# An attention-and-MLP kernel on one core: attention output computed token-major, 48 columns a head, and transposed afterwards

## The chip, the cores and the metric

The kernel runs on one core of a Trainium2 chip. Every time is in microseconds (us) on the device. The median of seven runs of the kernel before is 222.66 us (220.71 to 225.13). "PE" is the matrix engine (TensorE) and "PEld" its weight loads, "DVE" the vector engine, "ACT" the scalar engine, "POOL" GpSimd, and "SP" the sync engine, which here only issues DMAs. In a matmul one operand is loaded as weights and the other moves through the array; the number of moving columns is called its width.

## What is computed

There are two parts. The first is a gated linear attention over 4 sequences of 768 tokens, with 8 heads of 48 values; the second is a two-layer MLP with a sine-square activation on the result (d_model 384, d_ff 2048, 3072 tokens).

```python
f = 1.0 / (1.0 + np.exp(-f_logit))
for t in range(S):
    state = f[:, :, t, :, None] * state + np.einsum('bhd,bhe->bhde', k[:, :, t], v[:, :, t])
    y[:, :, t] = np.einsum('bhd,bhde->bhe', q[:, :, t], state)
x = y.transpose(0, 2, 1, 3).reshape(B * S, H * D)
h = x @ w_in
s = np.sin(alpha * h)
g = h + s * s / (alpha + 1e-09)
out = g @ w_out
```

Inputs and outputs are float32; the matmuls take bfloat16.

## The kernel before, in words

**Tiling.** The 768 tokens are cut into 6 chunks `c` of 128. A "unit" `u` is one chunk of two sequences, 12 in all; `m` counts the 24 pairs of chunk and sequence `b`. For each chunk all 4 sequences give one token block of 512 columns for the MLP; in chunk 0 alone the MLP works on two halves of 256.

**The gate phase, `pre` (from L326).** For a unit ACT takes exp and ln of the gate logits (L333, L336). For each `m`, PE sums the logs over tokens with a triangular mask (`cs`, L363 and, for the decay of the whole chunk, L366); ACT takes two exponentials of it (`Gi` L376, `G` L372); POOL or DVE multiplies k and DVE multiplies q (L385) into `qk`. DVE makes `v` bfloat16 (`values`, L342 to L347). exp and ln live in another activation table than the sine, so ACT switches tables (L628) between gate phases and sines; the list `PHASES` says when.

**The attention of a chunk, `attend`.** `tp` (L420) transposes k and q on PE and `tr` (L428) evicts them, in chunks 0 to 3; in chunks 4 and 5 a DMA transpose issued by SP does this (L426). `aps` (L437) is k against q, DVE masks it into `at` (L440). The output y is made of `inter` (L445, the carried state against q) and `intra` (L458, v against `at`); both leave it with **features on partitions**: the weights are the state or v, and the moving operand is 128 tokens wide. Two heads share a matmul and a head is padded from 48 to 64 rows, so the output comes in 4 blocks of 128 rows, and its rows don't lie as the MLP wants them. Hence `v_b` is stored padded, with zeros; `y_` (L465) evicts all 4 blocks into `xT`; and `spread` (L508) moves the fourth block's rows, in pieces of 16 partitions, into gaps of the other three, by 6 small DMAs a chunk from SP or POOL. For chunk 0 a second copy of v (`v1_b`) lets PE do this itself, with 12 matmuls instead of 8. The rows of `w_in` are loaded in the same order, in 16 DMAs (L295). `kv_` (L471, L473) adds the chunk's k times v to the state (the old state is added by an identity matmul, L471), and DVE scales it by the decay into `st` (L479).

**The MLP.** `first` makes h (PE, three matmuls of 512 columns, L529), the sine (ACT, L534), its square (POOL, ACT or DVE, L540 and L542) and g (DVE, L547). `second` sums 16 matmuls of 384 columns into o (L566), evicts it (L574) and stores it (L577).

**Order.** Nothing is left to a scheduler on the chip: `in_order` plans it while the program is built, from each operation's written durations, ranks (`RANK`, `ATT`, `LAG`, `KIND`), engine biases (`BIAS`) and rings of buffers (`R`), and then each engine runs its instructions in exactly that order. The loads follow the list `LOADS`; `W_GATE` names the loads after which POOL issues the weights. PSUM has three rings: 3 buffers for attention (`a`, shared by cs, tp, aps, y and kv), 3 for h, 2 for o. `NG` is the number of g tiles that may wait for o.

Of the kernel before, what the change touches and what calls it, by code (L numbers as in the profile page):

```python
# [17 lines left out]
NG = 36  # L18
PE_TR = 4
SPARE = 15  # L20
LOADS = [("k", 0), ("f", 0), ("q", 0), ("v", 0), ("f", 1), ("v", 1), ("q", 1), ("k", 1), ("f", 3),
    ("k", 3), ("f", 2), ("q", 3), ("q", 2), ("f", 5), ("v", 3), ("v", 2), ("k", 2), ("k", 4),
    ("f", 4), ("v", 4), ("q", 4), ("k", 5), ("v", 6), ("q", 5), ("k", 7), ("v", 7), ("f", 6),
    ("v", 5), ("k", 6), ("f", 7), ("q", 6), ("v", 10), ("f", 8), ("q", 7), ("q", 8), ("k", 8),
    ("v", 8), ("k", 11), ("v", 9), ("v", 11), ("f", 11), ("f", 9), ("k", 9), ("q", 10), ("k",
    10), ("q", 9), ("q", 11), ("f", 10)]
W_GATE = [1, 6, 15]
LAG = [389, 183, 51, 210, 208, 289]
ATT = [150, -130, -181, 58, -47, 55]
PHASES = [("pre", [0]), ("pre", [1]), ("sin", 16), ("pre", [2, 3]), ("sin", 15), ("pre", [4, 5]),  # L30
    ("sin", 17), ("pre", [6, 7, 8]), ("sin", 18), ("pre", [9, 10, 11]), ("sin", 46)]
RANK = [-6, 628, -691, -10, 175, 71, 8, 20, -437, -18, -103, -123]
MULS = {"POOL": 1020, "DVE": 750}
KIND = {"v": [147, 9, 46, 75, 127, -2],
        "cs": [-145, -32, -204, -182, -55, -258],
        "kh": [-179, -112, -104, -31, -147, -299],
        "qh": [-145, -50, -132, -383, -199, -136],
        "tp": [-133, -167, -186, -203, -128, -244],
        "tr": [116, 196, 76, 293, 139, 285],
        "a": [-282, -297, -247, -321, -246, -206],  # L40
        "m": [83, 264, 119, 421, 58, 182],
        "y": [-85, 152, 24, 75, 105, 196],
        "i": [81, 10, -86, -217, 109, 54],
        "kv": [148, 97, 59, 86, 61, 178],
        "st": [129, 130, -157, 126, 215, -54],
        "h": [5, -27, 43, 31, -36, -92],
        "sq": [114, 125, 112, 12, 253, 139],
        "g": [-119, 51, -134, 78, 119, -14],
        "ev": [-69, -174, -183, -117, -240, -203]}
SPREAD = {"SP": 1800, "POOL": 1600}  # L50
BIAS = {"ACT": 400, "DVE": 500, "POOL": 500, "SP": -1800}
# [12 lines left out]
class Op:  # L64
    after, line = 0, None
# [11 lines left out]
def in_order(ops, lines):  # L77
# [28 lines left out]
    while left:  # L106
        best = None
        for o in pending:
            if o.line and turn[o] != nth[o.line]:
                continue  # L110
            t = when(o)
            if t is None:
                continue
            for e, dur in o.engs.items():
                s = max(t, free[e])
                if o.dma:
                    s = max(s, dma_free[e] - DMA_AHEAD)
                d = dur + (TABLE_LOAD if o.table and o.table != table and table else 0)
                key = (s + (BIAS[e] if len(o.engs) > 1 else 0), o.rank, s + d)
                if best is None or key < best[0]:  # L120
                    best = (key, o, e, s, d)
# [28 lines left out]
def kernel(  # L150
# [18 lines left out]


# [3 lines left out]
    E = 64  # L174
# [7 lines left out]
    POS = (0, 3, 1, 2)  # L182
# [28 lines left out]
    def op(rank, engs, emit, deps=(), takes=(), holds=(), table=None, dma=None):  # L211
# [8 lines left out]
        h=N_H, s=3, s2=3, g=NG, o=2, osb=3).items()}  # L220
# [6 lines left out]
    v1_b = [consts.tile([C, 2, 2, 7, E], BF16, name=f"v1{i}") for i in range(2)]  # L227
    v_b = [consts.tile([C, HP, 2, 2, 2, E], BF16, name=f"vb{i}") for i in range(NV)]
# [21 lines left out]
    for i in range(max(NQ, NV)):  # L250
        for ts in (lf_b, v_b, v1_b, qk_b):
            if i >= len(ts):
                continue
            if ts is v_b:
                nc.vector.memset(ts[i], 0.0)
            elif ts is v1_b:
                nc.vector.memset(ts[i], 0.0)
            else:
                nc.vector.memset(ts[i].rearrange("c x y r e -> c (x y r) e")[:, :, D:], 0.0)
# [30 lines left out]
    def w_in_load(hf, rank):  # L290
        gate = weights_after(hf, rank)
        for j, p0, r0, n in ((0, 0, 0, E), (1, 0, 80, E), (2, 16, 3 * D, D), (2, 0, D + 16, 16)):
            for r in range(2):
                def emit(e, j=j, p0=p0, r0=r0, n=n, r=r):
                    nc.gpsimd.dma_start(out=w_in_bf[r * E + p0:r * E + p0 + n, j, HF[hf]],  # L295
                                        in_=moe_w_in[4 * D * r + r0:4 * D * r + r0 + n, HF[hf]])
                w_in_dma[hf].append(op(rank, {POOL: 550}, emit, deps=[gate],
                                       dma=830 if n == E else 620 if n == D else 210))
# [27 lines left out]
    def pre(u, rank):  # L326
        c = u // NU
# [11 lines left out]
        def values(e):  # L339
            vi = tl["v", u].rearrange("c (br p) d -> c p br d", p=HP)  # L340
            vo = v_b[bufs["vb", u].place % NV].rearrange("c p b r x e -> c p (b r) x e")
            nc.vector.tensor_copy(vo[:, 0:2, :, 0, :D], vi[:, 0:2])  # L342
            nc.vector.tensor_copy(vo[:, 2:4, :, 0, 16:], vi[:, 2:4])
            if u < NU:
                v1 = v1_b[u].rearrange("c b r x e -> c (b r) x e")
                nc.vector.tensor_copy(v1[:, :, 1, D:], vi[:, 1, :, :16])
                nc.vector.tensor_copy(v1[:, :, 3:6:2, :16], vi[:, 1, :, 16:].rearrange("c n (x d) -> c n x d", x=2))  # L347
# [4 lines left out]
        made["v", u] = op(rank + KIND["v"][c] + 2, {DVE: 1300 if u < NU else 1050}, values, deps=[vb_.ready], takes=[vv], holds=[vb_])  # L352
        late = []
        for i in range(2):
# [34 lines left out]
            c_ = op(rank + KIND["cs"][c] + i, {PE: 170 if last else 370}, cs_, deps=[l], takes=[cb], holds=[lf])  # L389
# [7 lines left out]
            made["kh", m] = op(rank + KIND["kh"][c] + i, MULS, km, deps=[gi, kb_.ready], takes=[qkb], holds=[kb_, Gib])  # L397
            made["qh", m] = op(rank + KIND["qh"][c] + i, {DVE: 490}, qm, deps=[g, qb_.ready], takes=[qkb], holds=[qb_, cb])
# [5 lines left out]
    def attend(c, b, rank):  # L404
        u, i = c * NU + b // 2, b % 2
        m = 2 * u + i
        first, last = c == 0, c == NCH - 1
        tpb, trb, ab, atb = c < PE_TR and buf("a"), buf("tr"), [buf("a"), buf("a")], [buf("at0"), buf("at1")]
        yb, kvb, sb = buf("a"), buf("a"), buf(f"st{b}")
# [31 lines left out]

        def inter_(e):
            y = tl[x, "y"] = ps_a.tile([P, HP, C], F32, tag="a", name=f"y_{c}_{b}")
            for p in range(HP):
                nc.tensor.matmul(y[:, POS[p], :], tl["st", c - 1, b][:, p, :, :].rearrange("d r e -> d (r e)"),  # L445
                                 tl[x, "tr"][:, HP + p, :], start=(p == 0), stop=False, skip_group_check=True)

        def intra_(e, r):
            if first and r == 0:
                tl[x, "y"] = ps_a.tile([P, HP, C], F32, tag="a", name=f"y_{c}_{b}")  # L450
            for p in range(HP):
                if first and p == 1:
                    v1 = v1_b[u][:, i, r].rearrange("c x e -> c (x e)")
                    vs = [(blk, v1[:, (2 * n + 1 - r) * E:(2 * n + 3 - r) * E]) for n, blk in enumerate((0, 2, 1))]
                else:
                    vs = [(POS[p], v_b[vb.place % NV][:, p, i].rearrange("c r x e -> c (r x e)")[:, r * E:(r + 2) * E])]
                for blk, v_ in vs:
                    nc.tensor.matmul(tl[x, "y"][:, blk, :], v_, tl[x, "at", r][:, p, :],  # L458
                                     start=(first and p == r == 0), stop=(r == 1), skip_group_check=True)

        def y_(e):
            if ("xT", c) not in tl:
                tl["xT", c] = xp.tile([P, HP, TOK], BF16, tag="xT", name=f"xT_{c}")
            n = KB if first else HP
            (nc.scalar.copy if e == ACT else nc.vector.tensor_copy)(  # L465
                tl["xT", c][:, :n, b * C:(b + 1) * C], tl[x, "y"][:, :n, :])

        def kv_(e):
            kv = tl[x, "kv"] = ps_a.tile([P, HP, 2, E], F32, tag="a", name=f"kv_{c}_{b}")
            if not first:  # L470
                nc.tensor.matmul(kv, ident, tl["st", c - 1, b], start=True, stop=False, skip_group_check=True)  # L471
            for p in range(HP):
                nc.tensor.matmul(kv[:, p, :, :], qk_b[qkb.place % NQ][:, 0, p, :, :].rearrange("c r e -> c (r e)"),  # L473
                                 v_b[vb.place % NV][:, p, i, :, 0, :],
                                 start=(first and p == 0), stop=True, skip_group_check=True)

        def st_(e):
            t = tl["st", c, b] = st_pool.tile([P, HP, 2, E], BF16, tag=f"s{b}", name=f"st_{c}_{b}")
            nc.vector.tensor_tensor(t, tl[x, "kv"], tl["gl", m].unsqueeze(3).to_broadcast([P, HP, 2, E]),  # L479
                                    Alu.mult)  # L480

        if c < PE_TR:
            kt = op(rank + KIND["tp"][c], {PE: 250}, lambda e: tp_(e, 0), deps=[made["kh", m]], takes=[tpb], holds=[qkb])
# [176 lines left out]
```

## Time and profile before

| | us |
|---|---|
| Median of seven runs | 222.66 |
| The profiled execution, its own time | 220.65 |
| Its span, first to last instruction | 218.9 |
| PE busy (85%), as the profile models ends | 187.1 |
| ACT busy (75%) | 165.1 |
| DVE busy (75%) | 164.5 |
| POOL busy (45%) | 99.6 |

The granted PE clock was 0.967 of full speed on average. The inputs are read in 48 loads of 384 KB by SP; they take most of the first 130 us. A busy share of PE counts the latency of each matmul, and so overstates how full PE is: the pitch, from one matmul's start to the next, is used below instead. The lines of the profile stand in the prediction.

### The profile page before, as it was taken

Reading aid. Unit: us, or ns where it says so; the run is one execution under the profiler, and the core shown is the slowest. Engines: PE = TensorE matmul, PEld = TensorE weight load, DVE = VectorE, ACT = ScalarE, POOL = GpSimd, SP = SyncE. Lnnn points to the kernel's source line nnn. Section 1 sums busy time; section 2 is a strip of 40 time slices with the busy share of each in tenths; the row PEclk is TensorE's granted clock in tenths of the full one; section 3 lists DMA queues with packets and bytes.
Section 4 is the critical chain, followed back from the end, with each engine's and each line's share of the span. In section 5 each row is a group of like instructions: output and inputs, shape, how many; then the busy total and the mean of one; then the engine's idle time right before and its main releaser. Section 6 shows DMA issues by size and latency. Waiting matters only on the chain.

```text
span 218.9 us, 4306 instructions
## 1 busy us (share of the span) xinstructions
PE 187.1 (85%) x1513; PEld 115.3 (53%) x1529; DVE 164.5 (75%) x301; ACT 165.1 (75%) x275; POOL 99.6 (45%) x134
## 2 busy tenths in 40 slices
PE   0259774888999898986899999999999999999993
PEld 0157552566675455643565654655665555555551
DVE  7677778568987999894589898669878858778700
ACT  2545949987689787899968889988877787777511
POOL 5721776176427454854633355465454642132300
PEclk9999999569999999999699999999999999999999
DMA  8999999999993999969699996555410101101111
GB/s 132 191 211 188 189 209 185 192 180 201 190 174 77 179 190 187 182 131 214 146 198 189 180 157 116 167 144 99 96 55 7 72 18 39 55 17 43 68 72 72
DMA packets 115125, 29.61 MB, mean 135 GB/s; under 512 B 108720, under 2 KB 114336, under 8 KB 115104
## 3 DMA queue, kind: packets, MB, share of 16 engines
q1 hardware_dynamic: 111648, 26.04, 67.0%
q0 software_dynamic: 3456, 3.30, 9.1%
q8 instruction: 12, 0.20, 0.4%
q14 instruction: 9, 0.07, 0.1%
HBM read 25.17 MB, written 4.72 MB: 137 GB/s over the span
## 4 chain that ended last, share of the span: by engine, by line
PE 57%; ACT 11%; DMA 10%; DVE 7%; SPq 5%; issue 5%; POOL 2%; ACTq 0%; POOLq 0%
PE o L566 24%; PE h L529 21%; SPq L271 5%; DMA q<-in_q_dram 4%; DMA w_out_bf<-in_moe_w_out_dram 3%; PE y L458 3%; DVE g L547 3%; DMA w_in_bf<-in_moe_w_in_dram 3%; ACT f L333 3%; PE aps L437 2%; ACT Gi L376 2%; PE y L445 2%; ACT L628 2%; POOL w_in_bf L295 2%; PE tp L420 2%
## 5 line engine op out<-in xcount | busy, mean ns | idle before, releaser
L542 POOL TENSOR_TENSOR s<-s 128x512 f32<-128x512 f32 (+1 forms) x65 | 58.5, 911 | 69.7 <-ACT s L534 57.9
L534 ACT ACTIVATE s<-h,al_p 128x512 f32<-128x512 f32 (+1 forms) x112 | 67.6, 628 | 25.3 <-PE h L529 22.8
L529 PE MATMUL h<-xT,w_in_bf 128*128 128x512 bf16 (+1 forms) x320 | 77.1, 355 | 6.7 <-DVE g L547 3.1
L547 DVE SCALAR_TENSOR_TENSOR g<-s,al_r,h 128x512 bf16<-128x512 f32 (+1 forms) x112 | 71.9, 665 | 12.4 <-POOL s L542 9.3
L566 PE MATMUL o<-w_out_bf,g 128*128 128x384 bf16 x384 | 78.1, 329 | 1.1 <-DMA w_out_bf<-in_moe_w_out_dram 1.1
L566 PEld LDWEIGHTS <-g 128*128 128x128 bf16 x384 | 36.5, 98 | 25.3 <-issue 1.6
L529 PEld LDWEIGHTS <-w_in_bf 128*128 128x128 bf16 x336 | 32.2, 100 | 29.7 <-issue 5.0
L440 DVE TENSOR_TENSOR at<-aps,mask 128x512 bf16<-128x512 f32 x48 | 31.4, 683 | 3.5 <-PE aps L437 3.2
L385 POOL TENSOR_TENSOR qk<-k,Gi 128x384 bf16<-128x384 f32 x22 | 21.6, 1002 | 17.7 <-ACT Gi L376 17.7
L540 ACT ACTIVATE s<-s 128x512 f32<-128x512 f32 (+1 forms) x36 | 20.8, 584 | 0.9
L385 DVE TENSOR_TENSOR qk<-q,cs 128x384 bf16<-128x384 f32 x24 | 13.2, 552 | 10.1 <-ACT cs L372 10.0
L363 PE MATMUL cs<-lf,mask 128*128 128x384 bf16 x24 | 9.0, 381 | 12.3 <-ACT lf L336 10.1
L458 PE MATMUL y<-at,vb 128*128 128x128 bf16 x184 | 18.5, 228 | 0.3 <-DVE at L440 0.3
L479 DVE TENSOR_TENSOR st<-kv,gl 128x512 bf16<-128x512 f32 x20 | 13.3, 683 | 5.4 <-PE kv L473 5.4
L420 PE MATMUL tp<-ident,qk 128*128 128x128 bf16 x128 | 12.1, 250 | 3.7 <-POOL qk L385 2.0
L574 ACT COPY osb<-o 128x384 f32<-128x384 f32 x16 | 7.7, 479 | 9.4 <-PE o L566 9.2
L333 ACT ACTIVATE f<-f 128x768 f32<-128x768 f32 x12 | 10.0, 836 | 5.9 <-POOL seen L287 5.1
L458 PEld LDWEIGHTS <-vb 128*128 128x128 bf16 x184 | 13.1, 103 | 2.4 <-issue 0.2
L376 ACT ACTIVATE Gi<-cs 128x384 f32<-128x384 f32 x24 | 11.6, 484 | 3.4 <-PE cs L366 2.7
L437 PE MATMUL aps<-tr 64*128 64x128 bf16 x192 | 10.5, 229 | 4.2 <-DVE tr L428 3.0
L420 PEld LDWEIGHTS <-qk 128*128 128x128 bf16 x128 | 9.9, 113 | 6.9 <-POOL qk L385 3.8
L465 ACT CAST xT<-y 128x512 bf16<-128x512 f32 (+1 forms) x20 | 11.2, 566 | 1.5 <-PE y L458 1.2
(56 smaller groups left out, 171.1 us busy)
## 6 DMA issues: line engine op xcount, KB each, us to landing
k<-in_k_dram SPq DMA_DIRECT2D x12, 384.0 KB, 6.6
f<-in_f_logit_dram SPq DMA_DIRECT2D x12, 384.0 KB, 6.7
q<-in_q_dram SPq DMA_DIRECT2D x12, 384.0 KB, 6.7
v<-in_v_dram SPq DMA_DIRECT2D x12, 384.0 KB, 6.8
out_dram<-osb SPq DMA_DIRECT2D x24, 192.0 KB, 1.9
w_out_bf<-in_moe_w_out_dram POOLq DMA_DIRECT2D x4, 384.0 KB, 7.6
w_in_bf<-in_moe_w_in_dram POOLq DMA_DIRECT2D x8, 128.0 KB, 5.5
w_in_bf<-in_moe_w_in_dram POOLq DMA_DIRECT2D x4, 96.0 KB, 6.2
```

The source lines that it names most:

```text
L333: nc.scalar.activation(out=tl["f", u], in_=tl["f", u], func=Act.Exp, scale=-1.0)
L376: nc.scalar.activation(out=tl["Gi", m], in_=tl["cs", m][:, :H * D], func=Act.Exp)
L385: engine[e].tensor_mul(qk_b[bufs["qk", m].place % NQ][:, "kq".index(n), :, :, :D], tl[n, u][:, i * H:(i + 1) * H, :].rearrange("c (r p) d ...
L420: nc.tensor.transpose(tl[x, "tp"][:, j * HP + p, :], qk_b[qkb.place % NQ][:, j, p, :, :].rearrange("c r e -> c (r e)"), ident)
L440: nc.vector.tensor_mul(tl[x, "at", r], tl[x, "a"][r], mask4)
L458: nc.tensor.matmul(tl[x, "y"][:, blk, :], v_, tl[x, "at", r][:, p, :], start=(first and p == r == 0), stop=(r == 1), skip_group_check=True)
L529: nc.tensor.matmul(h[:, :n], w_in_bf[:, kb, fs], xT[:, kb, ts], start=(kb == 0), stop=(kb == KB - 1))
L534: nc.scalar.activation(out=s[:, :n], in_=tl[x, "h"][:, :n], func=Act.Sin, scale=al_p[:, fb:fb + 1])
L540: nc.scalar.activation(out=s2[:, :n], in_=s[:, :n], func=Act.Square)
L542: engine[e].tensor_mul(s2[:, :n], s[:, :n], s[:, :n])
L547: nc.vector.scalar_tensor_tensor(tl["g", c, fb][:, ts], tl[x, "s2"][:, :n], al_r[:, fb:fb + 1], tl[x, "h"][:, :n], Alu.mult, Alu.add)
L566: nc.tensor.matmul(tl["o", c, t], tl["g", c, fb][:, t * P:(t + 1) * P], w_out_bf[:, fb, :], start=(fb == 0), stop=(fb == FB - 1))
```

## The change

The output of attention is now computed with **tokens on partitions**: `at` and the transposed q (`tr`) are the weights, and v (48 columns) or the state (96 columns, two heads) moves. A head needs no padding: v is one contiguous copy (`v_b` with H x 48 columns), the zeroing of `v_b` and `v1_b` at the start is gone, and so is `v1_b`. y is one tile of 128 x 384, evicted to `yn`. It must then be transposed for the MLP: in chunks 0 to 2 (`Y_TR = 3`) by three PE transposes into a PSUM buffer of ring `a` and an eviction `x_` by DVE or ACT, in chunks 3 to 5 by a DMA transpose from SP. x is in natural order, so `spread` is gone and `w_in` comes in 6 plain DMAs.

The state has 48 columns a head too. From chunk 2 on (`SUM = 2`) the identity matmul is gone: DVE adds the old state (`sum_`), and the scaling goes to POOL or DVE.

The numbers for the planner are all new, with values for each unit where there was one for each chunk, a bias for ACT (`ON_ACT`), another order of loads, another gate for weights, 44 g tiles in place of 36, and one gate phase more (that of units 6 to 8 is cut in two). In the instruction order of the built program POOL does all 12 scalings of the state that it may do, and ACT has 12 table loads where there were 10.

```diff
-NG = 36
+NG = 44
 PE_TR = 4
+Y_TR = 3
+SUM = 2
...
-W_GATE = [1, 6, 15]
+W_GATE = [4, 7, 14]
...
-PHASES = [("pre", [0]), ("pre", [1]), ("sin", 16), ("pre", [2, 3]), ("sin", 15), ("pre", [4, 5]),
-    ("sin", 17), ("pre", [6, 7, 8]), ("sin", 18), ("pre", [9, 10, 11]), ("sin", 46)]
+PHASES = [("pre", [0]), ("pre", [1]), ("sin", 18), ("pre", [2, 3]), ("sin", 14), ("pre", [4, 5]),
+    ("sin", 10), ("pre", [6]), ("sin", 6), ("pre", [7, 8]), ("sin", 16), ("pre", [9, 10, 11]),
+    ("sin", 48)]
...
-    v1_b = [consts.tile([C, 2, 2, 7, E], BF16, name=f"v1{i}") for i in range(2)]
-    v_b = [consts.tile([C, HP, 2, 2, 2, E], BF16, name=f"vb{i}") for i in range(NV)]
+    v_b = [consts.tile([C, 2, H, D], BF16, name=f"vb{i}") for i in range(NV)]
...
-            if ts is v_b:
-                nc.vector.memset(ts[i], 0.0)
-            elif ts is v1_b:
-                nc.vector.memset(ts[i], 0.0)
...
+        for kb in range(KB):
+            def emit(e, kb=kb):
+                nc.gpsimd.dma_start(out=w_in_bf[:, kb, HF[hf]], in_=moe_w_in[kb * P:(kb + 1) * P, HF[hf]])
...
+            nc.vector.tensor_copy(v_b[vv.place % NV].rearrange("c b h d -> c (b h) d"), tl["v", u])
...
         def inter_(e):
-            y = tl[x, "y"] = ps_a.tile([P, HP, C], F32, tag="a", name=f"y_{c}_{b}")
+            y_tile()
+            y = tl[x, "y"].rearrange("c (r p d) -> c p r d", r=2, p=HP)
             for p in range(HP):
-                nc.tensor.matmul(y[:, POS[p], :], tl["st", c - 1, b][:, p, :, :].rearrange("d r e -> d (r e)"),
-                                 tl[x, "tr"][:, HP + p, :], start=(p == 0), stop=False, skip_group_check=True)
+                nc.tensor.matmul(y[:, p], tl[x, "tr"][:, HP + p, :], tl["st", c - 1, b][:, p, :, :],
+                                 start=(p == 0), stop=False, skip_group_check=True)
         def intra_(e, r):
...
+                h = HP * r + p
+                nc.tensor.matmul(tl[x, "y"][:, h * D:(h + 1) * D], tl[x, "at", r][:, p, :],
+                                 v_b[vb.place % NV][:, i, h, :],
+                                 start=(first and p == r == 0), stop=(r == 1), skip_group_check=True)
...
+        def yt_(e):
+            if e == SP:
+                nc.sync.dma_start_transpose(xT(e), tl[x, "yn"].rearrange("c k d -> c (k d)"))
+                return
+            tl[x, "yt"] = ps_a.tile([P, KB, C], BF16, tag="a", name=f"yt_{c}_{b}")
+            for kb in range(KB):
+                nc.tensor.transpose(tl[x, "yt"][:, kb, :], tl[x, "yn"][:, kb, :], ident)
+        def x_(e):
+            (nc.scalar.copy if e == ACT else nc.vector.tensor_copy)(xT(e), tl[x, "yt"])
...
-            if not first:
+            if not first and c < SUM:
                 nc.tensor.matmul(kv, ident, tl["st", c - 1, b], start=True, stop=False, skip_group_check=True)
...
+        def sum_(e):
+            t = tl[x, "sum"] = at_pool.tile([P, HP, 2, D], F32, tag="sum", bufs=2, name=f"sum_{c}_{b}")
+            nc.vector.tensor_tensor(t, tl[x, "kv"], tl["st", c - 1, b], Alu.add)
+        def st_(e):
+            t = tl["st", c, b] = st_pool.tile([P, HP, 2, D], BF16, tag=f"s{b}", name=f"st_{c}_{b}")
+            engine[e].tensor_tensor(t, tl[x, "kv"] if c < SUM else tl[x, "sum"],
+                                    tl["gl", m].unsqueeze(3).to_broadcast([P, HP, 2, D]), Alu.mult)
...
-    def spread(c, rank):
-        def emit(e, r):
-            xT = tl["xT", c]
-            for blk, dst, src in ((0, D, 0), (2, 0, 16), (1, 0, 32)):
-                engine[e].dma_start(out=xT[r * E + dst:r * E + dst + 16, blk, :],
-                                    in_=xT[r * E + src:r * E + src + 16, 3, :])
...
+                nc.tensor.matmul(h[:, :n], w_in_bf[:, kb, fs], xT[:, ts.start // C:ts.stop // C, kb, :],
                                  start=(kb == 0), stop=(kb == KB - 1))
```

## The prediction

> **What bounds the kernel now.** I read the page's busy shares first, then the three rows of engines over 40 slices, then stretches cut at ACT's table switches, and last PE's order of time in the late part.
>
> ```profile
> PE   0259774888999898986899999999999999999993
> DVE  7677778568987999894589898669878858778700
> ACT  2545949987689787899968889988877787777511
> PE 57%; ACT 11%; DMA 10%; DVE 7%; SPq 5%; issue 5%; POOL 2%; ACTq 0%; POOLq 0%
> ```
>
> No engine is full for the whole span. From slice 21 (115 us) on PE is; before it ACT and DVE take turns. The chain that ended last says the same: 57% PE, most of it late. The stretches (length, then busy us of PE, PEld, DVE, ACT, POOL, granted clock, DMA, GB/s):
>
> ```profile
> 0.00:35.65 35.65, 19.46 (x177) 14.63 (x177) 26.09 (x61) 20.54 (x38) 19.41 (x46) 1.00 1.22 187
> 35.65:62.55 26.90, 21.70 (x209) 15.79 (x210) 20.27 (x45) 21.18 (x40) 12.70 (x20) 0.81 1.27 193
> 62.55:95.08 32.53, 30.25 (x278) 18.51 (x280) 30.10 (x51) 27.84 (x43) 17.75 (x20) 1.00 0.98 162
> 95.08:133.50 38.42, 34.26 (x286) 20.35 (x289) 30.78 (x59) 33.93 (x55) 18.76 (x22) 0.96 0.99 177
> 133.50:145.80 12.30, 12.25 (x91) 7.20 (x90) 8.20 (x17) 11.51 (x21) 6.34 (x8) 1.00 0.50 132
> 145.80:218.90 73.10, 69.14 (x479) 38.87 (x484) 49.09 (x72) 50.10 (x81) 24.59 (x24) 0.99 0.19 56
> ```
>
> PE's busy time includes latency, so I take pitches from its order of time (start, length, count):
>
> ```profile
> 159.01 0.40 PE L437 MATMUL aps<-tr 64*128 64x128 bf16 x8
> 159.34 0.40 PE L445 MATMUL y<-tr,st 128*128 128x128 bf16 x4
> 159.58 0.61 PE L458 MATMUL y<-at,vb 128*128 128x128 bf16 x8
> 160.03 0.81 PE L529 MATMUL h<-xT,w_in_bf 128*128 128x512 bf16 x3
> 160.67 0.39 PE L445 MATMUL y<-tr,st 128*128 128x128 bf16 x4
> 162.64 1.30 PE L566 MATMUL o<-w_out_bf,g 128*128 128x384 bf16 x7
> 163.78 0.81 PE L529 MATMUL h<-xT,w_in_bf 128*128 128x512 bf16 x3
> ```
>
> From one start to the next: h 0.64/3 = 0.214 us (other places 0.216, which I use), o 1.14/7 = 0.1625, y of L458 0.45/8 = 0.056, aps 0.33/8 = 0.041. With these, all PE work is 170 us. The last mask matmul `cs` starts at 144.49; what PE has after it is 129 h x 0.216, 208 o x 0.1625, 56 aps x 0.041, 101 narrow ones x 0.056 and a few wide: 69.9 us. PE's last matmul ends at 215.3, so 70.8 us passed. PE is the bound there, within 1 us.
>
> Before that it isn't: PE has 99.9 us of work in 144.5. ACT's instructions, counted in order with their mean durations, make 123.2 us to the end of its last gate phase at 145.8: 22.6 us of idle, of which 13.3 lie before the first switch back at 35.65. After it ACT idles 9.3 us in 110. So stage 1 (to 144.5) is ACT's, with the start; stage 2 (70.8) PE's; then an eviction and a store (3.6), and 1.75 outside the span.
>
> **The change, stage 1.** *ACT* in the new order, to the same point: 2 table loads more (+2.6), 1 `tr` more (+1.0), evictions of y 15 x 0.484 in place of 3 x 0.484 and 10 x 0.581 (0), 4 evictions of transposes (rows: 0.484 for 384 f32 columns, 1.011 for 1024 bf16; I take 0.48: +1.9), 2 sines fewer (-1.4), 9 squares fewer (-4.6: they go to POOL or past this point), 5 evictions of o fewer (-2.4, to DVE). Sum -2.9: 120.3.
>
> *The start.* exp of the gates began when the second load had landed:
>
> ```profile
> 7.18 0.84 ACT L333 ACTIVATE f<-f 128x768 f32<-128x768 f32 x1 [5.08 <-POOL seen L287]
> ```
>
> Now f is the first load. 384 KB at 190 GB/s are 2.0 us: -2.0. The zeroing of v (4 x 0.912 + 2 x 0.805 = 5.2 us of DVE) ran to 7.8, beside the wait for the load; gone, it leaves DVE free when an earlier load needs it, so it is no second gain. The first half of `w_in` now waits for the 5th load in place of the 2nd, but by issues of 3 x 0.6 us in place of 8 x 0.5; I expect it near 21 us, as the first h needs it now (21.46), and the second half near 29 (30.77). Cost 0, up to +2 if late.
>
> *The new step* from y to x in chunk 0: 3 transposes at 0.056 with a latency near 0.25, then an eviction (DVE: between 0.26, in proportion to 0.682 for 1024 bf16, and 0.557 for 384 f32; I take 0.35) with a wait at each end: about +1.0 once before the first sines. In chunks 1 and 2 the sines of the chunk before cover it.
>
> *Idle after the start.* DVE's work to the same point falls from 128.4 to about 117: zeroing -5.2; v copies 24 in two kinds (0.58 on average, and the `v1_b` copies) to 12 of about 0.75, -5.7; state steps 20 x 0.683 to 18 x 0.55 so far, -3.8 (12 scalings go to POOL at 1.0, the row of its 384-column multiply; the state is needed a chunk later, so that is covered); x +2.1; o evictions +2.2; others -1. PE's work falls from 99.9 to 95.3. ACT waits for PE's h, which waits for buffers that DVE frees (ACT waited for h 19 times in 36 to 146 us, 9.8 us in all). Bounds: 0 to -5 of the 9.3; I take a quarter, -2.2.
>
> One v copy rests on a rule. The Trainium skill ("SBUF — State Buffer", section on the two sides) says that DVE in a two-port mode and GpSimd hold a shared port for a whole instruction, and the other blocks. The trace agrees, and prices it:
>
> ```profile
> 11.13 1.02 POOL L385 TENSOR_TENSOR qk<-k,Gi 128x384 bf16<-128x384 f32 x1
> 11.25 1.14 DVE L342 CAST vb<-v 128x384 bf16<-128x384 f32 x1
> 12.31 0.35 DVE L343 CAST vb<-v 128x384 bf16<-128x384 f32 x1
> ```
>
> Two equal copies, 1.14 beside POOL's multiply and 0.35 after it. Twice the columns[...] add 0.2: 0.55 alone, and 1.3 if each meets a POOL instruction. POOL gets 12 state scalings more. At the bad end the copies give back 12 x 0.55 = 6.6 us of DVE, and my -2.2 with it.
>
> Stage 1: -2.9 - 2.0 + 1.0 - 2.2 = -6.1, so 138.4. Could the loads forbid it? SP's last load left at 128.7; to 130 us the core moved 23.1 MB, at 195 GB/s 118 us of it. Twelve us of slack.
>
> **Stage 2.** After its last `cs` the new PE order has 135 h, 204 o, 48 aps, 48 of `intra`, 24 of `inter`, 8 of kv; two chunks of y, the last `kv` included. Widths are 48 and 96. For 96 columns I scale to 0.0425. For 48 the ends are: 0.056 (no gain), and 0.025, the pitch of the one-column matmuls:
>
> ```profile
> 99.91 0.24 PE L366 MATMUL cs<-ones_c,lf 128*128 128x1 bf16 x4
> ```
>
> (one lasts 0.164, so 0.076 for three steps). I take 0.041, as aps has a weight load for each matmul at that pitch. Sum: 29.2 + 33.2 + 2.0 + 2.0 + 1.0 + 0.5 = 67.8 us, -2.1; over the whole kernel 163.1 for 169.8, of which the 12 identity matmuls fewer give 2.8 and the 36 transposes take 2.0. A rule speaks against this: the Trainium skill ("TensorE: Matmul & The Clock Gate", section on LDWEIGHTS) prices a load at its columns over 1.2 GHz, 107 ns for 128, whatever the width that follows. Then 192 `intra` matmuls would take 20.5 us and not 7.9: +12.6, of which 48 x 0.066 = 3.2 in stage 2. But the rows above show 128-column loads every 0.041 and 0.056 us, so I hold to the row.
>
> DVE has more in stage 2: 57.2 us for 51.5 (4 o evictions, 3 y, 2 g, 2 sums more). Before, the 51.5 took 61.6 us to its last g, 10 idle, and PE ran on for 7 us behind it. With 1.1 after the last g, 56 in about 61 leave 5 idle: +0.7. The DMA transposes of chunks 3 to 5 (issue 1.26, landing 3.2 for 1024 columns, 384 here) stand in place of `spread`'s six issues (3.7 for six, landing 1.8); SP has little else to do then, and h of the chunk before covers them: 0. Stage 2: -1.4, so 69.4.
>
> **Sum.** 138.4 + 69.4 + 3.6 + 1.75 = 213.2 against the profiled 220.65. The median stands 2.0 above that: **215.2**.
>
> **Rivals.**
> *The idle goes away* (0.18). ACT's 9.3 us fall to about 2, with -5 more than I take, since both engines that it waits for are relieved. Then 210. For: DVE at 30.1 of 32.5 in 62 to 95 us. Against: gate phases have idle of their own ("issue", 0.4 us at a time).
> *Nothing gained before stage 2* (0.13). ACT's order hardly changes its work, and if v copies and the later weights eat the start, only -1.4 stays: 221, or 223 with one late weight.
> *PSUM's ring becomes the bound: slower* (0.17). Ring `a` still has 3 buffers, now with a 7th user per chunk and sequence in chunks 0 to 2. A transposed y holds one until DVE or ACT, both in fixed order, evict it; `cs`, `tp` and `aps` queue on PE behind that, and ACT's gate phase behind `cs`. At 1 us for each of 12 that is +12: 227. It decides from 7.4/12 = 0.6 us each. For: DVE's queue is near full just there. Against: the v and state steps leave it.
>
> **How the numbers follow.** Main case 0.52, 212 to 219. A difference below 0.5% (1.1 us) is about what this kernel's times can't tell from none. Faster: main, the first rival and half of the second, 0.76; within 0.5%: 0.07; slower 0.17. Range: 209 leaves under a tenth below; 225 takes in the lesser stalls of the ring.
>
> **What would show it.** exp starting near 5.2; the last `cs` at 138 to 139 and PE's end 69 us later; `intra` of eight matmuls in 0.33 us (0.45 or 0.85 would be the other two prices); evictions of `yt` below 0.5 us on DVE; v copies of 0.55 at their least. Wrong if the last `cs` comes after 144, or if PE shows idle time on `yt`'s eviction.

## The result, and the profile after

The changed kernel takes 218.94 us (median of 12 runs, 217.36 to 221.07); the kernel before, beside it, 222.51. The ratio is 0.986 (95% interval 0.9825 to 0.9895): 1.4% faster, where 3.3% was forecast. 218.9 lies in the range, but 3.7 us above the 215.2. Medians take in every execution; ratios, here and below, leave out the slow ones (one of the 12 here, three of six in `w_dve`), so the two can differ.

The two traces differ by less than the medians: the profiled execution of after took 220.5 us (span 218.8), near the slow end of its runs, and that of before 220.65, at the fast end of its runs. So stretches are compared one by one below, and whole kernels by their medians and ratios.

The rows of engines over 40 slices and the chain that ended last, of after:

```profile
PE   0468646736999988896999989997999999999993
DVE  2387862737689579988969998749899968787820
ACT  3565443897479997698998898998898888687601
PEclk9999975885799999999999999999999999999999
PE 52%; ACT 13%; DVE 9%; DMA 9%; POOL 6%; SPq 5%; issue 5%; ACTq 0%; POOLq 0%
```

and the row of the granted PE clock of before:

```profile
PEclk9999999569999999999699999999999999999999
```

Late in the span little has changed. What is new stands in the 5th to 7th digit (22 to 38 us): ACT at 4, 4 and 3 where it was at 9, 4 and 9, PE at 6, 4 and 6 where it was at 7, 7 and 4, and a clock of 7 and 5 from the 6th digit on. The dip at 5 and 7 further on (49 to 60 us) is not new: before has one at 5 and 6, two slices earlier. In the chain PE has lost 5 points, POOL has gained 4, ACT and DVE 2 each. The stretches, cut at ACT's table switches as before (start:end, length, then busy us of PE, PEld, DVE, ACT, POOL, granted clock, DMA share, GB/s):

```profile
0.00:41.65 41.65, 22.49 (x199) 15.97 (x200) 23.96 (x59) 21.38 (x40) 17.79 (x39) 0.88 1.17 179
41.65:146.28 104.63, 92.04 (x879) 55.64 (x879) 83.33 (x158) 90.67 (x147) 62.20 (x71) 0.95 1.06 176
144.97:215.25 70.28, 68.97 (x470) 36.90 (x467) 53.90 (x83) 52.27 (x85) 21.52 (x22) 1.00 0.22 60
```

and the last two of them for the kernel before, whose first stretch (0 to 35.65) the prediction shows:

```profile
35.65:145.80 110.15, 98.46 (x859) 61.85 (x869) 89.34 (x169) 94.45 (x158) 55.55 (x67) 0.94 1.00 171
144.49:215.30 70.81, 70.44 (x489) 39.74 (x494) 50.21 (x74) 50.92 (x84) 25.72 (x25) 1.00 0.19 55
```

That is the result in five rows. The gate phases (second stretch) became 5.5 us shorter, as forecast. Stage 2 became 0.5 shorter. And the first stretch, forecast at 34.7, became 41.65: ACT has only 0.8 us more work in it and 5.2 us more idle time than before. Where that idle time ends is in the order of time of POOL, PE and ACT, of after:

```profile
24.66 0.17 POOL L286 COPY seen<-v 1x1 f32<-1x1 f32 x1 [5.83 <-DMA v<-in_v_dram]
24.78 0.60 POOL L293 DMA_DIRECT2D w_in_bf<-in_moe_w_in_dram  x1
25.39 0.89 POOL L556 TENSOR_TENSOR s<-s 128x256 f32<-128x256 f32 x1
26.24 0.59 POOL L293 DMA_DIRECT2D w_in_bf<-in_moe_w_in_dram  x1
26.85 0.62 POOL L556 TENSOR_TENSOR s<-s 128x256 f32<-128x256 f32 x1
27.41 0.59 POOL L293 DMA_DIRECT2D w_in_bf<-in_moe_w_in_dram  x1
...
33.99 0.40 PE L543 MATMUL h<-xT,w_in_bf 128*128 128x256 bf16 x1 [3.70 <-DMA w_in_bf<-in_moe_w_in_dram]
35.33 5.70 PE L543 MATMUL h<-xT,w_in_bf 128*128 128x256 bf16 x28 [0.94 <-DMA w_in_bf<-in_moe_w_in_dram]
...
26.32 0.47 ACT L548 ACTIVATE s<-h,al_p 128x256 f32<-128x256 f32 x1 [2.50 <-POOL s L556]
...
35.82 0.47 ACT L548 ACTIVATE s<-h,al_p 128x256 f32<-128x256 f32 x1 [5.19 <-PE h L543]
```

and of before:

```profile
21.01 0.17 POOL L287 COPY seen<-q 1x1 f32<-1x1 f32 x1 [8.86 <-DMA q<-in_q_dram]
21.25 4.10 POOL L295 DMA_DIRECT2D w_in_bf<-in_moe_w_in_dram  x8
...
30.77 0.61 PE L529 MATMUL h<-xT,w_in_bf 128*128 128x256 bf16 x4 [1.28 <-DMA w_in_bf<-in_moe_w_in_dram]
```

The second half of `w_in` waits, on POOL, for a load that marks when it may go. That was q1, the 7th load, seen at 21.01. Now it is v1, the 8th, seen at 24.66. The squares of the sines stand in POOL's order behind that copy and between the three issues. The gate opens 3.65 us later. The three issues, with the squares between them, take 3.2 us where the eight took 4.1, so the last one leaves 2.65 us later (28.0 in place of 25.35). And from there to PE's last wait for `w_in` it is 7.3 us in place of 5.4: the rows of `w_in` needed by block 8 arrive at 33.99 to 35.33 in place of 30.77. PE stands still for 3.70 us. ACT stands still twice: 2.50 us for a square that had to wait behind the copy on POOL, and 5.19 us for h.

The delay then grows, by PE's clock. Windows of after and, last, of the run `a_quarters` below (columns as above):

```profile
30.00:34.00 4.00, 0.30 (x2) 0.01 (x1) 1.38 (x4) 0.60 (x2) 0.00 (x0) 0.93 1.02 169
35.33:41.03 5.70, 5.70 (x28) 4.02 (x29) 3.75 (x9) 4.03 (x9) 3.88 (x7) 0.55 1.29 195
```

```profile
32.57:34.20 1.63, 1.59 (x13) 1.28 (x14) 0.31 (x1) 1.31 (x4) 0.76 (x2) 1.00 0.85 174
```

The 28 matmuls that had been held up ran at 0.204 us each, with a granted clock of 0.55; the same shape took 0.122 (13 in 1.59) at a clock of 1.00 in `a_quarters`, where PE's wait just before them was 1.37 us. 28 x 0.08 = 2.3 us is my estimate of what the clock cost, as ACT's last ten sines of the chunk went at PE's pace; no run takes the clock alone. The Trainium skill ("TensorE: Matmul & The Clock Gate", Part 1 on the clock gate) says the clock is halved after an idle window of about 3.4 us; the 3.70 us here fit it. But these traces show no such threshold: in after the clock was at 0.50 from 27 to 30 us too, behind a wait of 1.86 us.

### The profile page after: what moved, and what is told of

The parts are those of the page before. It is cut to its first block, busy times and chain, and to the rows that moved or that the text cites. A ratio compares the mean times of both kernels' runs of the same rounds, so it can differ in the third digit from the quotient of the medians.

```text
span 218.8 us, 4284 instructions
## 1 busy us (share of the span) xinstructions
PE 182.2 (83%) x1537; PEld 107.7 (49%) x1537; DVE 160.4 (73%) x297; ACT 163.5 (75%) x269; POOL 100.2 (46%) x129
## 4 chain that ended last, share of the span: by engine, by line
PE 52%; ACT 13%; DVE 9%; DMA 9%; POOL 6%; SPq 5%; issue 5%; ACTq 0%; POOLq 0%
PE o L581 23%; PE h L543 21%; DMA v<-in_v_dram 5%; SPq L270 5%; DVE g L561 4%; POOL s L556 4%; DMA w_in_bf<-in_moe_w_in_dram 4%; ACT L643 3%; ACT s L548 3%; ACT Gi L364 2%; DVE at L429 2%; PE aps L426 2%; ACT lf L331 1%; ACT f L328 1%; PE tp L409 1%
## 5 line engine op out<-in xcount | busy, mean ns | idle before, releaser
L543 PE MATMUL h<-xT,w_in_bf 128*128 128x512 bf16 (+1 forms) x336 | 79.5, 362 | 9.8 <-DMA w_in_bf<-in_moe_w_in_dram 4.8
L543 PEld LDWEIGHTS <-w_in_bf 128*128 128x128 bf16 x336 | 33.1, 102 | 36.7 <-issue 7.1
L581 PEld LDWEIGHTS <-g 128*128 128x128 bf16 x384 | 35.8, 98 | 23.5 <-issue 0.7
L351 PE MATMUL cs<-lf,mask 128*128 128x384 bf16 x24 | 8.1, 357 | 10.0 <-ACT lf L331 8.6
L446 PE MATMUL y<-vb,at 128*128 128x48 bf16 x192 | 11.5, 187 | 5.0 <-DVE vb L335 3.1
L446 PEld LDWEIGHTS <-at 128*128 128x128 bf16 x192 | 8.9, 98 | 11.2 <-DVE at L429 5.2
L426 PE MATMUL aps<-tr 64*128 64x128 bf16 x192 | 11.0, 228 | 2.6 <-ACT tr L417 1.5
L556 DVE TENSOR_TENSOR s<-s 128x512 f32<-128x512 f32 (+1 forms) x11 | 7.8, 708 | 7.2 <-ACT s L548 7.1
L417 ACT COPY tr<-tp 128x1024 bf16<-128x1024 bf16 x10 | 9.9, 1019 | 3.9 <-PE tp L409 3.9
L409 PEld LDWEIGHTS <-qk 128*128 128x128 bf16 x128 | 10.4, 118 | 4.9 <-POOL qk L373 2.6
```

The costliest lines, as they stand in the source:

```text
L409: nc.tensor.transpose(tl[x, "tp"][:, j * HP + p, :], qk_b[qkb.place % NQ][:, j, p, :, :].rearrange("c r e -> c (r e)"), ident)
L446: nc.tensor.matmul(tl[x, "y"][:, h * D:(h + 1) * D], tl[x, "at", r][:, p, :], v_b[vb.place % NV][:, i, h, :], start=(first and p == r == 0 ...
L543: nc.tensor.matmul(h[:, :n], w_in_bf[:, kb, fs], xT[:, ts.start // C:ts.stop // C, kb, :], start=(kb == 0), stop=(kb == KB - 1))
L556: engine[e].tensor_mul(s2[:, :n], s[:, :n], s[:, :n])
L581: nc.tensor.matmul(tl["o", c, t], tl["g", c, fb][:, t * P:(t + 1) * P], w_out_bf[:, fb, :], start=(fb == 0), stop=(fb == FB - 1))
```

## The experiments

| run | what it is | us | ratio to before (95%) | second switch | last `cs` |
|---|---|---|---|---|---|
| before | | 222.5 to 223.1 | 1 | 35.65 | 144.49 |
| after | | 218.94 | 0.986 (0.9825 to 0.9895) | 41.65 | 144.97 |
| `a_unsplit` | after, three issues together | 218.31 | 0.9805 (0.9753 to 0.9857) | 39.94 | 142.34 |
| `a_gate` | after, gate q1, issues together | 216.27 | 0.9731 (0.9681 to 0.9781) | 38.46 | 140.86 |
| `a_quarters` | after, gate q1, in two parts | 215.32 | 0.9661 (0.9628 to 0.9693) | 36.56 | 140.08 |
| `b_late` | before, second half of `w_in` late | 227.09 | 1.0203 (1.0151 to 1.0255) | 41.34 | 149.71 |
| `layout_old_numbers` | new layout, planner's numbers of before | 244.65 | 1.0983 (1.0926 to 1.104) | | |
| `w_wide` | after, narrow matmuls twice | 221.94 | 0.9965 (0.9937 to 0.9993) | 41.54 | 146.31 |
| `w_memset` | after, zeroing put back | 220.89 | 0.9915 (0.9886 to 0.9943) | 42.41 | 145.73 |
| `w_dve` | after, zeroing and more v copies | 222.75 (218.93 to 225.99) | 0.9898 (0.984 to 0.9957) | 39.95 | 144.91 |
| `q_memset` | `a_quarters`, zeroing put back | 215.62 | 0.9719 (0.9661 to 0.9777) | 34.87 | 138.32 |
| `q_copy` | `a_quarters`, more v copies | 218.82 | 0.9851 (0.9787 to 0.9915) | 37.42 | 142.22 |

The last two columns are of each run's profiled execution.

My theory: the new layout gives what was forecast, and the late second half of `w_in` takes half of it away. The rivals: the start is late for another reason (DVE, or loads), or the layout's gain is small.

**The gate alone.** `a_unsplit` keeps the gate v1 and only takes the squares from between the issues:

```diff
-                nc.gpsimd.dma_start(out=w_in_bf[:, kb, HF[hf]], in_=moe_w_in[kb * P:(kb + 1) * P, HF[hf]])
+                for j in [kb] if hf == 0 else range(KB) if kb == 0 else []:
+                    nc.gpsimd.dma_start(out=w_in_bf[:, j, HF[hf]], in_=moe_w_in[j * P:(j + 1) * P, HF[hf]])
```

> The kernel after, its plan kept, the gate of the second half of w_in kept at v1, but its three DMAs issued together at once, ahead of POOL's squares. Theory: they are issued 1.4 us earlier (by 26.6 in place of 28.0), h of the second half starts 1 to 1.5 us earlier, but the first squares 1.2 us later; time 0.5 to 1.5 us below the kernel after, 217.5 to 218.5. Rival (loads as a whole): no change.

It measured 218.31, as the theory had it, but its interval overlaps that of after. `a_gate` has that and takes the name of before's gate, q1. Here q1 is the 5th load, not the 7th, and has long landed: POOL passes the copy at 18.9 us, when its order comes to it, 2 us before the gate of before:

```diff
-        return op(rank, {POOL: 100}, lambda e: nc.gpsimd.tensor_copy(seen[:, i:i + 1], tl[n, u][0:1, 0, 0:1]),
+        r = LOADS[W_GATE[0]] if i == 1 else (n, u)
+        return op(rank, {POOL: 100}, lambda e: nc.gpsimd.tensor_copy(seen[:, i:i + 1], tl[r][0:1, 0, 0:1]),
```

> The kernel after, its whole plan kept, with the second half of w_in released by the load q1 (already there at 13.4 us) and its three DMAs issued together, in place of waiting for v1 (24.6 us) and being issued between POOL's squares. Theory (the late second half of w_in ate the gain: ACT stood 2.5 us behind POOL's wait and 5.2 us behind h): the last mask matmul moves from 145.0 to about 140, time 3 to 6 us below the kernel after's 218.9, so 213 to 216; v1 comes some 4 us later and takes part of it back. Rival (the loads as a whole set the pace of stage 1, so it does not matter in which order they come): last mask matmul stays within 1 us of 145, time 218 to 220.

It measured 216.27. Nothing of the plan but this gate and these issues differs, and 2.7 of the missing 3.7 us are back, clear of after's interval: the theory holds, and the gate is the larger part of it. One cost came along. The weights now go out among the loads, and v1 came late. Of `a_gate`, a line of DVE's order of time, and then two of its waits between 24 and 40 us (total, times, longest):

```profile
27.94 0.56 DVE L337 CAST vb<-v 128x768 bf16<-128x768 f32 x1 [2.61 <-DMA v<-in_v_dram]
```

```profile
PE y L448 <- DVE vb L337: 5.3, 2, 4.1
ACT yn L454 <- PE y L448: 5.2, 3, 4.2
```

Chunk 0's y waited for that v. Hence `a_quarters`: at the gate q1 only the columns of blocks 8 to 11, then two squares on POOL, then those of blocks 12 to 15.

```diff
+                quarter = d_ff // 4
+                parts = [(kb, HF[hf])] if hf == 0 else []
+                if hf == 1 and kb != 1:
+                    a = d_ff // 2 + (quarter if kb else 0)
+                    parts = [(j, slice(a, a + quarter)) for j in range(KB)]
+                for j, cols in parts:
+                    nc.gpsimd.dma_start(out=w_in_bf[:, j, cols], in_=moe_w_in[j * P:(j + 1) * P, cols])
```

> The kernel after, its plan kept, with w_in's second half released by q1 as in the first of these runs, but only its columns for blocks 8 to 11 at once, and those for 12 to 15 two POOL instructions later. Theory (the weights and v1 compete for the DMA engines, and in the first run v1 came at 27.9 in place of 24.6 and held y, and ACT behind it): v1 comes 1.5 us or so earlier than in the first run and nothing waits for blocks 12 to 15; 0.5 to 1.5 us below its 216.3. Rival (the bytes needed by 35 us are the limit, in whatever order): 216 to 217.

It measured 215.32, 3.4% under before and the fastest kernel of all here. The copy of v1 began at 25.06 us, for 24.82 in after and 27.94 in `a_gate`. Its first two stretches:

```profile
0.00:36.56 36.56, 19.48 (x199) 14.28 (x200) 23.50 (x59) 20.91 (x41) 19.52 (x42) 1.00 1.16 181
36.56:141.39 104.83, 92.06 (x879) 55.59 (x879) 82.07 (x158) 90.64 (x147) 62.15 (x71) 0.95 1.15 183
```

The gate phases are as long as in after (104.63), and so is stage 2 (70.3). The first stretch is 5.1 us shorter, and that is the whole difference between the two profiled executions (215.61 for 220.5). Its POOL and its PE (order of time):

```profile
18.91 0.17 POOL L287 COPY seen<-q 1x1 f32<-1x1 f32 x1
19.03 1.66 POOL L300 DMA_DIRECT2D w_in_bf<-in_moe_w_in_dram  x3
23.47 1.18 POOL L563 TENSOR_TENSOR s<-s 128x256 f32<-128x256 f32 x2 [2.78 <-ACT s L555]
24.60 1.66 POOL L300 DMA_DIRECT2D w_in_bf<-in_moe_w_in_dram  x3
...
30.91 0.28 PE L550 MATMUL h<-xT,w_in_bf 128*128 128x256 bf16 x1 [0.43 <-DMA w_in_bf<-in_moe_w_in_dram]
32.57 1.59 PE L550 MATMUL h<-xT,w_in_bf 128*128 128x256 bf16 x13 [1.37 <-DMA w_in_bf<-in_moe_w_in_dram]
```

**The same in the kernel before.** If late weights are what costs, then they must cost it there too. `b_late` has before's layout and plan, with the second half behind f3, two loads later:

```diff
-        return op(rank, {POOL: 100}, lambda e: nc.gpsimd.tensor_copy(seen[:, i:i + 1], tl[n, u][0:1, 0, 0:1]),
+        r = LOADS[8] if i == 1 else (n, u)
+        return op(rank, {POOL: 100}, lambda e: nc.gpsimd.tensor_copy(seen[:, i:i + 1], tl[r][0:1, 0, 0:1]),
```

> The kernel before, its plan kept, with the second half of w_in released two loads later (f3 in place of q1, about 25 in place of 21 us). Theory: the second half lands 4 us later, near 35 as in the kernel after, and ACT's first sines with it; time 3 to 5 us above the kernel before, 225.5 to 227.5. Rival: no change, 222.5.

It measured 227.09. Of b_late, POOL's order of time:

```profile
25.52 0.17 POOL L288 COPY seen<-f 1x1 f32<-1x1 f32 x1 [13.28 <-DMA f<-in_f_logit_dram]
25.76 4.10 POOL L296 DMA_DIRECT2D w_in_bf<-in_moe_w_in_dram  x8
```

A gate at 25.52 in place of 21.01, 4.5 us later, put the second switch 5.7 us later, the last `cs` 5.2, and the time up by 4.3. The start isn't cushioned in either kernel. What an earlier or a split gate would give the kernel before was not run, so how much of the 3.4% of `a_quarters` is the layout's own stays open.

**The layout without its plan.** `layout_old_numbers` is the new layout planned with before's `LOADS`, `W_GATE`, `PHASES`, `LAG`, `ATT`, `RANK`, `BIAS` and `NG`; `KIND` has each value twice, the new kinds `yt` and `xe` take those of y, and `ON_ACT` is 0.

> The new layout of the kernel after (48 columns a head, transposes, natural x, sums) planned with the numbers of the kernel before (loads, gates, ranks, phases, biases, 36 g tiles; the new steps get the rank of y). Theory (the layout itself lowers the work of DVE by some 10 us and of PE by 7): faster than the kernel before although nothing is tuned to it, 215 to 219. Rival (the gain is the new plan's, and the layout gives nothing without it): 221 us or more.

It measured 244.65, the rival's side, but for a reason that neither had named. SP's order of time, and then the page's row of GB/s in 40 slices:

```profile
91.99 30.66 SPq L587 DMA_DIRECT2D out_dram<-osb  x8
124.37 1.27 SPq L457 DMA_TRANSPOSE xT<-yn  x1
125.75 0.53 SPq L265 DMA_DIRECT2D k<-in_k_dram  x1
```

```profile
GB/s 138 192 198 194 189 190 188 188 192 204 200 188 181 192 171 222 0 32 1 69 102 201 178 187 164 159 9 151 104 58 82 50 81 35 32 32 32 67 66 65
```

In this plan eight stores of the output stand in SP's queue ahead of the loads that the next gate phase needs, and each waits for an o that comes late: the loads stop from 92 to 125 us. So this run says that the old numbers don't suit the layout, and nothing of what the layout alone is worth.

**The narrow matmuls.** `w_wide` issues each of the 192 matmuls of `intra` a second time, into columns that nobody reads, which makes a pair cost about what one cost before.

```diff
+                nc.tensor.matmul(tl[x, "y2"][:, H * D:], tl[x, "at", r][:, p, :],
+                                 v_b[vb.place % NV][:, i, h, :],
+                                 start=False, stop=(r == 1), skip_group_check=True)
```

> The kernel after, its plan kept, with each of the 192 matmuls of v issued a second time with the same weights, into columns of y's bank that nobody reads; two of them cost PE 0.05 us, about what one 128-column matmul of the kernel before cost. Theory (PE is the bound of stage 2, and little of stage 1): 48 extra ones in stage 2 add 1.2 us there, the other 144 (3.6 us) add up to 1 in stage 1; 1 to 2.5 us above the kernel after, 220 to 221.5. Rival (stage 2 has become DVE's, so the narrow matmuls are worth nothing): within 0.5 us of 218.9.

It measured 221.94: 3.0 us more by the medians, 2.3 by the ratios, a little over the expectation. The second copies are 192 x 0.025 = 4.8 us of PE, so half or more of it shows. In the profiled executions the last `cs` comes 1.3 later, in a stage where PE is not the bound but ACT waits for it, and stage 2 grew by 0.8 for its 48 copies (1.2 us).

**DVE's relief.** `w_memset` puts 5.2 us of zeroing back (a tile that nobody reads); `w_dve` has it too and copies half of each v a second time.

```diff
+    zero = consts.tile([C, 2048], BF16)
-        for ts in (lf_b, qk_b):
-            if i < len(ts):
+        for ts in (lf_b, 2048, 1792, qk_b):
+            if isinstance(ts, int):
+                if i < {2048: 4, 1792: 2}[ts]:
+                    nc.vector.memset(zero[:, :ts], 0.0)
+            elif i < len(ts):
...
+            nc.vector.tensor_copy(again.rearrange("c (h d) -> c h d", d=D), tl["v", u][:, :H, :])
```

> The kernel after, its plan kept, with the 5.2 us of zeroing that the kernel before did on DVE at its start put back (into a tile that nobody reads). Theory (the zeroing lay beside the wait for the first loads, and the first sines wait for w_in): 0 to 0.7 us slower, 218.9 to 219.6. Rival (the first gate phase now comes early enough to wait for it, and the delay is carried on): 1.5 to 3 us slower.

> As the run with the zeroing, and half of each v copy (384 columns, 0.35 us alone) done a second time into a tile that nobody reads, as the kernel before did two copies a unit; with waits for POOL 4 to 8 us more work for DVE, nearly all in stage 1. Theory (DVE's relief lets ACT idle less in stage 1): 1.5 to 3.5 us above the kernel after, 220.5 to 222.5. Rival (DVE's relief is worth nothing in stage 1, which waits for ACT and for loads): less than 1 us above.

`w_memset` measured 220.89, 2.0 more by the medians and 1.2 by the ratios: the rival's side at first sight. In its trace v1's gate opened at 25.21 in place of 24.66. `w_dve` decided nothing: its runs spread from 218.9 to 226.0. So both were done again, one by one, on `a_quarters`, where the weights are not late.

> The 5.2 us of zeroing on DVE put back, on the plan whose second half of w_in comes early (a_quarters, 215.3 us). Theory: DVE is late already when the first units need it, so zeroing costs about 2 us wherever the weights land: 216.8 to 217.8 us. Rival: in the changed kernel it cost 2 us only because it pushed v1, and with it the gate, later; with another gate it costs 0 to 0.7: 215.3 to 216.0.

> Half of each v copy done a second time on DVE, into a tile that nobody reads, on the plan whose second half of w_in comes early (a_quarters, 215.3 us): 12 more copies of 0.35 us, more beside POOL, some 4 to 8 us of DVE spread over the gate phases. Theory (the relief of DVE is what took the 2.2 us of idle time out of the gate phases): about a third of it comes back as time, 216.5 to 218 us. Rival (the idle time went for another reason, DVE's slack covers the copies): 215.3 to 216.0.

`q_memset` measured 215.62 for 215.32 (by the ratios, whose intervals overlap, 1.3 more): the rival's side by the medians. In its profiled execution, the fastest of its runs, the second switch is not later but earlier, at 34.87. So the zeroing seems to cost little where v1 isn't the gate; between 0 and 1.3 us these runs can't tell. `q_copy` measured 218.82: 3.5 us more for 12 copies of 0.504, 6.1 us of DVE.

```profile
L344 DVE CAST again<-v 128x384 bf16<-128x384 f32 x12 | 6.1, 504 | 0.0
```

More than half of it comes back as time, in the first stretch (+0.9) and the gate phases (104.83 to 106.11) in the profiled execution, which was the fastest of its runs. It is beyond the 216.5 to 218 expected, on the theory's side. POOL's instructions took no longer for it (101.9 us busy in both). So before stage 2 DVE is no spare engine.

## Why the prediction was wrong

The step that failed is the end of the part on the start: "I expect it near 21 us, as the first h needs it now (21.46), and the second half near 29 (30.77). Cost 0, up to +2 if late." The first half did come near 22. The second half came at 33.99 to 35.33, 3 to 5 us later than before instead of 2 earlier. I had costed the gate of the first half, by its place among the loads and by its issues, and carried the result over to the second. But the second has its own gate, v1, the 8th load where q1 had been the 7th, and that load landed 3.65 us later; its last issue took 7.3 us to land instead of 5.4; and its rows meet a PE whose clock has dropped. In the profiled execution the first stretch, forecast at 34.7, took 41.65: 7.0 us more, of which 0.8 is work of ACT and the rest waiting, where the term had 0, or 2 if late. `W_GATE` stands in the diff, and the trace of before shows the same gate opening at 21.01: the check was to count. By the medians the gate and the three issues are worth 2.7 (`a_gate`), and with the weights in two parts 218.94 - 215.32 = 3.6 (`a_quarters`), about the miss of 3.7. The last `cs` at 144.97 is beyond the 144 that the prediction named as its sign of being wrong.

The other steps, in the prediction's order:

- *ACT's work -2.9, idle time -2.2.* To the end of the last gate phase ACT was busy 115.0 us before and 112.05 after, -2.9: right (+0.8 in the first stretch, -3.8 after it). Its time without work behind the first stretch went from 15.70 to 13.96, -1.7 for -2.2: near. But the 9.3 us from which that was taken were too few. ACT's work of 123.2 us was a sum of durations, and the records of successive instructions overlap: the same stretch of the trace has 115.0 us in which ACT is busy. `q_copy` supports the reason given for the idle time: a loaded DVE brings it back.
- *exp near 5.2.* It began at 4.87 (7.18 before), and the first sine 2.1 us earlier than before, at 22.31 for 24.45. So the start itself was right, and what was lost was lost behind it:

```profile
4.87 0.84 ACT L328 ACTIVATE f<-f 128x768 f32<-128x768 f32 x1 [2.78 <-DMA f<-in_f_logit_dram]
```

- *Zeroing: no second gain.* Not refuted: 0.3 us by the medians and 1.3 by the ratios in `q_memset`; in the changed kernel 1.2 to 2.0, with v1 as the gate.
- *Costs of single steps*, groups of after (count, busy us, mean ns, idle before):

```profile
L335 DVE CAST vb<-v 128x768 bf16<-128x768 f32 x12 | 9.5, 788 | 0.6 <-DMA v<-in_v_dram 0.6
L469 DVE COPY xT<-yt 128x384 bf16<-128x384 bf16 x8 | 2.5, 348 | 0.0
L469 ACT COPY xT<-yt 128x384 bf16<-128x384 bf16 x4 | 1.9, 478 | 0.2
L486 POOL TENSOR_TENSOR st<-sum,gl 128x384 bf16<-128x384 f32 x12 | 10.1, 851 | 5.4 <-DVE sum L482 5.4
```

  The evictions of `yt` hit 0.35 and 0.48. A v copy took 0.556 at the median, as said for one alone; beside POOL up to 2.25, mean 0.788, near the 0.75 of the sum. POOL's scaling took 0.85 for 1.0.
- *Width 48 at 0.041 us.* Too dear. PE's order of time, and the group of the weight loads:

```profile
157.46 0.34 PE L438 MATMUL y<-st,tr 128*128 128x96 bf16 x4
157.64 0.36 PE L446 MATMUL y<-vb,at 128*128 128x48 bf16 x8
157.84 0.32 PE L581 MATMUL o<-w_out_bf,g 128*128 128x384 bf16 x1
```

```profile
L446 PEld LDWEIGHTS <-at 128*128 128x128 bf16 x192 | 8.9, 98 | 11.2 <-DVE at L429 5.2
```

  Eight matmuls, each with a load of 128 columns, in 0.20 us: 0.025 each, the lower bound; the four of 96 columns took 0.045 each for the 0.0425 of the sum. The Trainium skill's price for a load ("TensorE: Matmul & The Clock Gate", section on LDWEIGHTS), 107 ns for 128 columns, is near the 98 ns that one load lasts here. What does not hold is to take it as the pitch, from which the +12.6 came that the prediction set aside: 192 loads of 98 ns keep PEld busy for 8.9 us and not for 18.8, so their records overlap.
- *Stage 2: 69.4.* It took 70.28. PE's share without work rose from 0.37 to 1.31 us, about the +0.7 said for DVE, in waits that stage 2 of before has none of (total, times, longest):

```profile
PE y L446 <- DVE at L429: 0.7, 2, 0.5
PE h L543 <- DVE g L561: 0.4, 2, 0.3
```

  But with the cheaper pitch PE's own sum is 67.0, so 2.0 us more are not explained; no run was made for them. Start by start, nearly all the time over the pitches lies where PE changes to or from the short groups of `aps`, `y` and `kv`, and 0.3 us between o and h.
- *The rivals.* PSUM's ring: no wait of PE on an eviction of `yt` in the trace, and the kernel is not slower. Refuted. *Nothing gained before stage 2* had the number of the profiled execution (last `cs` at 144.97 for 144.49; 220.5 us for its 221) and part of the reason, the later weights; but the gate phases did gain 5.5 us, which the first stretch lost again. It had 0.13, and the median shows about half of the gain. *The idle goes away*: 13.96 of 15.70 remain.

That `a_quarters` lands on 215.3 beside the 215.2 is in part luck: its first stretch is 1.9 longer than forecast, stage 2 0.9, and its median lies 0.3 below its profiled execution, where I had added 2.0.

## What to carry to other kernels

When a diff renumbers a list of gates or loads, work out for each gate on its own which load opens it and when the trace shows that load landing, and what stands behind it in that engine's fixed order; one such number, with the order of the issues behind it, was worth 2.7 us here, beside the 3.6 that the redesigned layout and its plan gave without them. A gate that is a copy on an engine with other work holds up that work as well: POOL stood for 5.83 us. And where PE is left to wait, ask what clock it comes back to: behind the 3.70 us here it was 0.50 to 0.55, and the matmuls that ACT needed took 0.204 us instead of 0.122.

## What was not expected of the hardware

Matmuls with 48 moving columns and a fresh 128 x 128 weight load each follow each other every 0.025 us, no slower than the one-column matmuls of before, though each load lasts 0.098 us. Three issues of 256 KB by POOL took 1.67 us together in `a_gate`, 0.56 each, and 3.2 us (24.78 to 28.0) in after, with two squares between them. A DMA transpose of 128 x 384 bf16 in SBUF took 2.4 us from issue to landing at the median (3.2 for 1024 columns), and the trace of after shows no wait for one.
